# Unpermuted first chunk, one early load of the probabilities, first weights after the last q load, attention of later chunks moved up by six steps

## The chip, the cores and the metric

The kernel runs on one core of one Trainium2 chip. The metric is the device time of one execution in microseconds (us); the span in a profile, from the first to the last instruction, is 1.7 to 3.0 us shorter. Most executions agree within a per cent. Some come out 7 to 12 us later than the rest; they are called slow or late here, counted apart, and never used to explain a difference between fast ones.

## The reference

```python
# B=4, H=8, S=768, D=48; then N=3072 tokens, Din=384, E=4 experts, F=1024
f = 1.0 / (1.0 + np.exp(-f_logit))
for t in range(S):                      # gated linear attention
    state = f[:, :, t, :, None] * state + np.einsum('bhd,bhe->bhde', k[:, :, t], v[:, :, t])
    y[:, :, t] = np.einsum('bhd,bhde->bhe', q[:, :, t], state)
x = y.transpose(0, 2, 1, 3).reshape(B * S, H * D)
p = domain_probs / (domain_probs.sum(-1, keepdims=True) + 1e-09)
for e in range(E):                      # every expert, weighted by p
    out += p[:, e:e+1] * (np.maximum(x @ w1[e], 0.0) @ w2[e])
```

## The kernel before

The sequence is cut into 6 chunks of 128 steps. Each chunk goes through attention (gates, state sum "cs", products of q and k with exponentials, transposes, masked scores, y, transposed activations xT) and then through four experts of two layers. A list scheduler in Python simulates the engines with assumed durations, gives each step to an engine and fixes the order of all queues. The order on chip is what this simulation found.

```python
def load(c, nm, b, n):                                  # f, k, q, v: rows of 48 floats, 192 bytes
    ins[c, nm, b] = nc.sync.dma_start(out=tl(nm, c, b // 2)[:, hh(b, n), :], in_=srcs[nm][c, :, b * H:(b + n) * H, :])
def load_w(i, e, which):                                # expert weights, cast to bf16 on the way
    ins["w", i] = nc.gpsimd.dma_start(out=w[:, e], in_=r[e])
    if i == 0:
        after(ins["w", 0], ins[0, "k", B - 1])          # first weights wait for the first chunk's last k
# ... the first chunk's sixteen loads, in this order:
"f0 k0 q0 f1 k1 q1 f2 f3 k2 q2 v0 k3 q3 v1 v2 v3"
# ... tiles that stand ahead of the load buffers in SBUF:
pt = const.tile([128, B * C, E], FP32)                  # 384 bytes a partition
pn = const.tile([128, B * C, E], FP32)
psm = const.tile([128, B * C, 1], FP32)
# ... the plan's costs of a product (VectorE or GpSimd, whichever is free):
pe = {"DVE": 0.6, "POOL": 1.0} if c < 2 else {"POOL": 1.0}
```

## Time and profile before

| what | before |
|---|---|
| times | 301.59, 303.09 and 309.1 us, median 303.09 |
| span of the profiled execution | 300.35 us, clock 1.000 |
| first weights: issue, landing | 14.72, 23.05 us |
| head, up to the first expert matmul | 23.10 us |
| body, from there to the last matmul's end | 274.10 us |
| tail | 3.15 us |
| stops of TensorE in the body | 0.60 + 0.20 us at 80 to 82 us |

Head, body and tail add up to the span. A stop is a gap between the starts of two matmuls beyond what the first needs; gaps of 0.22 us that return regularly are lost records. The lines behind this table stand in the prediction.

### The profile page before, as it was taken

What the parts mean: (1) busy time and instruction counts of PE and PEld (TensorE: products, weight loads), DVE (VectorE), ACT (ScalarE), POOL (GpSimd) and SP (SyncE); (2) the same over time, 40 slices, a digit from 0 to 9 for tenths busy, and PEclk for the clock granted to TensorE, in tenths of its full rate; (3) what the DMA queues carried; (4) which work ended last, traced back from release to release, by engine and by line L of the source; (5) the groups of instructions that cost most, each with busy time, mean ns of one, the idle gap of its engine ahead of it and who ended that gap; (6) DMA issues with size and microseconds to landing.
All of it is one profiled execution on the core that took longest, in us unless ns stands there. A gap on an engine that the chain in (4) does not pass through costs nothing.

```text
span 300.4 us, 5514 instructions
## 1 busy us (share of the span) xinstructions
PE 290.7 (97%) x2111; PEld 168.1 (56%) x2141; DVE 135.8 (45%) x268; ACT 172.5 (57%) x300; POOL 95.7 (32%) x157
## 2 busy tenths in 40 slices
PE   7799999999999999999999999999999999999995
PEld 5564555567775565555555555555555555555553
DVE  6784013787852675516465325454415343201223
ACT  5766654858875455677355576445475444475440
POOL 4484400408756048423426243522432000000000
PEclk9999999999999999999999999999999999999999
DMA  7999999964994679969796978201322201200002
GB/s 155 210 180 206 207 207 200 220 103 71 224 208 103 119 142 180 196 136 156 152 177 116 241 147 153 49 21 34 94 58 52 48 13 41 75 4 2 0 0 105
DMA packets 137354, 36.08 MB, mean 120 GB/s; under 512 B 128496, under 2 KB 135792, under 8 KB 137328
## 3 DMA queue, kind: packets, MB, share of 16 engines
q1 hardware_dynamic: 131568, 29.45, 50.5%
q0 software_dynamic: 5760, 6.29, 12.6%
q8 instruction: 16, 0.26, 0.4%
q14 instruction: 10, 0.08, 0.1%
HBM read 31.51 MB, written 4.72 MB: 121 GB/s over the span
## 4 chain that ended last, share of the span: by engine, by line
PE 90%; DMA 4%; SPq 3%; DVE 1%; issue 1%
PE ps_m L356 42%; PE ps_m L344 41%; SPq L222 3%; DMA w_sb<-in_moe_w_dram 3%; PE ps_t L300 2%; DMA k<-in_k_dram 1%; PE ps_t L315 1%; PE ps_t L311 1%; PE ps_t L321 1%; PE ps_t L255 1%; PE ps_t L285 1%; DVE Sf L328 0%; DVE o L367 0%; DVE yb L218 0%; PE ps_t L340 0%
## 5 line engine op out<-in xcount | busy, mean ns | idle before, releaser
L356 PE MATMUL ps_m<-w_sb,h 128*128 128x384 bf16 x776 | 153.1, 324 | 0.2
L344 PE MATMUL ps_m<-xT,w_sb 128*128 128x512 bf16 (+1 forms) x594 | 150.8, 362 | 2.4 <-DMA w_sb<-in_moe_w_dram 0.5
L352 ACT ACTIVATE h<-ps_m 128x512 bf16<-128x512 f32 (+1 forms) x169 | 97.2, 577 | 96.5 <-PE ps_m L344 91.8
L356 PEld LDWEIGHTS <-h 128*128 128x128 bf16 x776 | 73.6, 98 | 58.7
L363 DVE SCALAR_TENSOR_TENSOR o<-ps_m,pn,o 128x384 f32<-128x384 f32 (+1 forms) x73 | 44.6, 611 | 107.3 <-PE ps_m L356 102.7
L344 PEld LDWEIGHTS <-w_sb 128*128 128x128 bf16 x624 | 59.5, 98 | 46.8 <-issue 0.8
L276 POOL TENSOR_TENSOR qk<-q,e 128x384 bf16<-128x384 f32 x19 | 22.8, 1202 | 67.3 <-ACT e L262 64.8
L335 POOL TENSOR_TENSOR Sf<-Sf,egs 48x192 f32<-48x192 f32 x40 | 20.1, 502 | 47.1 <-DVE Sf L328 45.1
L350 DVE TENSOR_SCALAR h<-ps_m 128x512 bf16<-128x512 f32 (+1 forms) x39 | 21.9, 578 | 27.6 <-PE ps_m L344 25.2
L304 DVE TENSOR_TENSOR AT<-ps_t,mask 128x512 bf16<-128x512 f32 x48 | 30.2, 682 | 6.8 <-PE ps_t L300 6.8
L276 POOL TENSOR_TENSOR qk<-k,e 128x384 bf16<-128x384 f32 x20 | 21.9, 1093 | 10.7 <-ACT egs L266 6.6
L262 ACT ACTIVATE e<-ps_t 128x384 f32<-128x384 f32 x24 | 20.8, 865 | 3.6 <-PE ps_t L255 2.5
L328 DVE TENSOR_TENSOR Sf<-Sf,ps_t 48x192 f32<-48x192 f32 x40 | 14.0, 350 | 8.3 <-PE ps_t L321 7.4
L336 POOL CAST sb<-Sf 48x192 bf16<-48x192 f32 x40 | 13.6, 339 | 2.6
L365 ACT ACTIVATE o<-ps_m,pn 128x384 f32<-128x384 f32 x20 | 11.6, 580 | 4.4 <-PE ps_m L356 3.2
L569 PE MATMUL ps_m<-busy 128*128 128x256 bf16 x69 | 12.1, 319 | 1.3 <-DVE busy L140 1.3
L264 ACT ACTIVATE e<-ps_t 128x384 f32<-128x384 f32 x24 | 13.0, 542 | 0.0
L247 ACT ACTIVATE ex<-f 128x768 f32<-128x768 f32 (+1 forms) x14 | 10.5, 750 | 4.4 <-DMA f<-in_f_logit_dram 4.4
L315 PE MATMUL ps_t<-vb,AT 128*128 128x48 bf16 x192 | 11.4, 184 | 1.0 <-DVE vb L218 1.0
L218 POOL CAST vb<-v 128x384 bf16<-128x384 f32 x18 | 9.4, 540 | 8.5 <-DMA v<-in_v_dram 7.3
L315 PEld LDWEIGHTS <-AT 128*128 128x128 bf16 x192 | 9.8, 97 | 3.1 <-issue 1.1
L251 ACT ACTIVATE gp<-ex 128x768 bf16<-128x768 f32 (+1 forms) x14 | 10.5, 752 | 0.4
(50 smaller groups left out, 134.5 us busy)
## 6 DMA issues: line engine op xcount, KB each, us to landing
w_sb<-in_moe_w_dram POOLq DMA_DIRECT2D x8, 768.0 KB, 18.9
out_dram<-o SPq DMA_DIRECT2D x23, 192.0 KB, 2.1
f<-in_f_logit_dram SPq DMA_DIRECT2D x10, 384.0 KB, 4.3
k<-in_k_dram SPq DMA_DIRECT2D x10, 384.0 KB, 5.5
q<-in_q_dram SPq DMA_DIRECT2D x10, 384.0 KB, 5.4
v<-in_v_dram SPq DMA_DIRECT2D x10, 384.0 KB, 5.1
f<-in_f_logit_dram SPq DMA_DIRECT2D x4, 192.0 KB, 4.0
k<-in_k_dram SPq DMA_DIRECT2D x4, 192.0 KB, 4.1
```

Of the source, the lines that this page charges most:

```text
L262: nc.scalar.activation(out=e[:, 0].rearrange("t (d h) -> t h d", d=D), in_=cs[:, 0:HD].rearrange("t (i r d) -> t r i d", r=2, d=D), func=A ...
L276: engines[eng].tensor_tensor(out=tl("qk", c, b)[:, j, :, 0:D].rearrange("t (i r) d -> t i r d", r=2), in0=tl("qk"[j], c, b // 2)[:, hh(b), ...
L304: nc.vector.tensor_tensor(out=tl("AT", c, b)[:, r].rearrange("s i t -> s (i t)"), in0=tl("A", c, b, r).rearrange("s i t -> s (i t)"), in1= ...
L315: nc.tensor.matmul(out=y[:, h * D:(h + 1) * D], lhsT=AT[:, r, i, :], rhs=vb[:, h, :], start=(c == 0), stop=True, skip_group_check=True)
L328: nc.vector.tensor_tensor(out=Sf[rows, b], in0=Sf[rows, b], in1=KV[rows, :, r, :], op=ALU.add)
L335: nc.gpsimd.tensor_tensor(out=Sf[rows, b], in0=Sf[rows, b], in1=eg, op=ALU.mult)
L336: nc.gpsimd.tensor_copy(out=nb[rows, b, :, r * D:(r + 1) * D], in_=Sf[rows, b])
L344: nc.tensor.matmul(out=tl("hp", c, e, fc, n0)[:, n0:n1], lhsT=w1_sb[:, e, kk, fc * 128:(fc + 1) * 128], rhs=tl("xT", c)[:, kk, n0:n1], sta ...
L350: nc.vector.tensor_relu(out=dst, in_=src)
L352: nc.scalar.activation(out=dst, in_=src, func=AF.Relu)
L356: nc.tensor.matmul(out=tl("op", c, e, nt, part)[:, cols], lhsT=tl("h", c, e)[:, fc, nt * T:(nt + 1) * T], rhs=w2_sb[:, e, fc, cols], start ...
L363: nc.vector.scalar_tensor_tensor(out=o, in0=op, scalar=pe, in1=o, op0=ALU.mult, op1=ALU.add)
```

## The change

The intent: finish the first chunk's attention earlier, keep the first weights out of the way of its last loads, take the small probability work out of the expert layers, and start later attention earlier.

```diff
-    pt = const.tile([128, B * C, E], FP32)
-    pn = const.tile([128, B * C, E], FP32)
-    psm = const.tile([128, B * C, 1], FP32)
+    NR = B * C
+    praw = const.tile([NR, T, E], FP32)            # 2048 bytes a partition
+    ident32 = const.tile([NR, NR], FP32)
+    pn = const.tile([T, E, NR], FP32)
+    psm = const.tile([T, NR], FP32)
@@ first weights
-            after(ins["w", 0], ins[0, "k", B - 1])
+            after(ins["w", 0], ins[0, "q", B - 1])
@@ probabilities: six loads by SyncE and six normalisations become one
+        nc.scalar.dma_start(out=praw, in_=moe_domain_probs.rearrange("(r p) e -> r p e", p=T))
+        for e in range(E):
+            nc.tensor.transpose(out=tl("pp")[:, e], in_=praw[:, :, e], identity=ident32)
@@ first chunk's exponential unpermuted
+        if c == 0:
+            nc.scalar.activation(out=e[:, 0], in_=cs[:, 0:HD], func=AF.Exp, scale=-1.0)
@@ the last batch's copies in parts (q/k, y and xT); here y
+            parts = [slice(0, KD)] if c or b < B - 1 else [slice(0, 2), slice(2, KD)]
@@ attention of chunks 4 to 6
-            base = u0 + (0 if c else 10)
+            base = u0 + {0: 10, 1: 0}.get(c, -6)
... (helpers, costs of the plan, lists of dependences: cut)
```

## The prediction

> **What bounds the kernel now.** I read the page's busy table first, then the sliced rows, the chain of waits, and the timeline around each place where TensorE stands still.
>
> ```profile
> PE 290.7 (97%) x2111; PEld 168.1 (56%) x2141; DVE 135.8 (45%) x268; ACT 172.5 (57%) x300; POOL 95.7 (32%) x157
> ...
> PE   7799999999999999999999999999999999999995
> ...
> PEclk9999999999999999999999999999999999999999
> DMA  7999999964994679969796978201322201200002
> ```
>
> TensorE is busy from the third slice to the end at full clock, every other engine is below 60%. But a busy PE need not be a useful one: the digits of the first three slices (to 22.5 us) are mostly filler matmuls on a tile "busy" that only keep the clock up. So there are three parts: a head until the first expert matmul, a body in which TensorE is the bound, and a tail.
>
> The chain of waits, cut to the head, says what the head waits for:
>
> ```profile
> 10.03 4.38 DMA k<-in_k_dram
> 14.72 8.33 DMA w_sb<-in_moe_w_dram
> 23.54 1.03 PE ps_m L344 x4
> ```
>
> The last k of the first chunk lands at 14.41; GpSimd, which waited for it, then issues the first expert weight slab, which lands at 14.72 + 8.33 = 23.05. The timeline of TensorE has the first expert matmul 0.05 us later:
>
> ```profile
> 21.68 0.34 PE L340 MATMUL ps_t<-ident,yb 128*128 128x128 bf16 x3
> 21.85 0.71 PE L569 MATMUL ps_m<-busy 128*128 128x256 bf16 x5
> 23.10 1.47 PE L344 MATMUL ps_m<-xT,w_sb 128*128 128x512 bf16 x5 [0.54 <-DMA w_sb<-in_moe_w_dram]
> ```
>
> The other condition, the last transposed activations (xT), is met at 22.53 (ACT copy at 22.05, 0.48 long). So the weights hold the end of the head, and attention is only 0.52 us behind them.
>
> The body: 6 chunks x 4 experts are 576 matmuls of 512 columns and 768 of 384. In the chain, four 384-column matmuls take 0.65 us (0.1625 each) and three 512-column ones 0.65 (0.216 each): 576 x 0.216 + 768 x 0.1625 = 249.2 us. From 23.10 to the end of the last matmul (297.2) are 274.1 us; the other 25 are attention's own matmuls for chunks 2 to 6. Going from start to start through TensorE's timeline I find, beside regular 0.22 us steps that are lost records (594 and 776 recorded where 624 and 768 or a few more were issued), just one real stop, of 0.6 us at 80.6:
>
> ```profile
> 79.59 0.17 DVE L241 TENSOR_REDUCE psm<-pt 128x4 f32<-128x16 f32 x1
> 79.80 0.17 DVE L242 TENSOR_SCALAR psm<-psm 128x4 f32<-128x4 f32 x1
> 80.01 0.18 DVE L243 RECIPROCAL psm<-psm 128x4 f32<-128x4 f32 x1
> 80.22 0.27 DVE L244 TENSOR_TENSOR pn<-pt,psm 128x16 f32<-128x16 f32 x1
> 80.52 1.14 DVE L367 TENSOR_SCALAR o<-ps_m,pn 128x384 f32<-128x384 f32 x2
> ...
> 81.19 1.01 PE L344 MATMUL ps_m<-xT,w_sb 128*128 128x256 bf16 x6 [0.43 <-DVE o L367]
> ```
>
> The second chunk's four small probability operations stand on VectorE ahead of the eviction that frees a PSUM buffer, and TensorE waits for that buffer. The tail, 297.2 to 300.4, is the last eviction and store.
>
> **What the Trainium skill says.** "PSUM — Partial Sum Buffer", section "Engine vs sequencer instructions": the queues of ScalarE, VectorE and GpSimd are strict FIFO. The lines above agree: the eviction at 80.52 stands behind 0.93 us of arithmetic on a few elements. "Advanced Engine Details and Errata", section "SBUF Cachelines": different 16-byte lines on each access cost time. The first chunk's exponential written in permuted order (a step of 32 bytes) takes 862 ns against 536 for the same size unpermuted, and the product that reads it permuted 856 on VectorE against 540: it agrees. "DMA: Bandwidth & Descriptors", section "Why small descriptors are slow (HBM only)": a packet carries a fixed overhead whatever its size. The 8 KB of one chunk's probabilities go as 512 rows of 16 bytes, and the transfer needs 10.5 us to land while the first weights move: no proof, but it agrees. "TensorE: Matmul & The Clock Gate", section "Wait — 56ns, not 53.3ns?": columns / 2.4 GHz plus 2.5 ns, so 162.5 and 215.8 ns; the trace agrees to the digit.
>
> **The change, part by part.**
> 1. First chunk unpermuted: 4 exponentials lose 0.33 us each on ScalarE, 4 q products 0.32 each on VectorE. Per batch the chain shortens by about 0.65 us. From arrival of the last q, VectorE is the pacing engine in this stretch (last mask product ends at 20.62).
> 2. Split copies for the last batch: the transposed q/k copy (1.01 us on ACT) becomes two of about 0.55, so the k half goes before q arrives; the y copy (0.54) and the xT copy (0.48) become two parallel parts, saving about 0.15 each. With 1, the last xT is ready at about 21.5 instead of 22.53 (estimate, adding the durations above behind the last q and v). That is 1.0 us off a path that is not the last one.
> 3. First weights now wait for the last q rather than the last k: those land at 15.32 and 14.41, so the issue slips by 0.9, and by about 0.25 more because the probabilities now go first (48 KB at some 200 GB/s). Against that: the old first slab moved its first packet at 16.62, while rows of v were still on the same 16 queues until about 17.1, and its packets took 0.7 to 0.8 us there instead of 0.172; and 512 probability packets of 22 ns, now gone, ran among it (some 400 before 22 us: 400 x 22 ns / 16 = 0.55 us). New sum, all from the packet records: issue 15.9, first packet 1.9 later at 17.8, about 0.6 of start-up, 340 packets at 100 per us = 3.4, so 21.9, and 0.3 to 1.0 until the slowest of the 16 engines has reported (one was held by an instruction fetch of 1.3 us at 16.1): **landing 22.2 to 22.9 or a little later, I take 22.7**, against 23.05. Gain 0.35.
> 4. The first state product of TensorE (4 matmuls of 96 columns, 0.17 us) now stands before the first expert matmul and falls into the wait for weights: 0.17 gained.
> 5. Probabilities: one load of 24 rows x 2 KB in the first microseconds on ScalarE's queue, four small transposes on TensorE where filler stood, and one normalisation for all chunks in the head in place of six. The operations between the chunks leave VectorE (5 x about 0.75 us). Only one of them was on the path: the 0.6 us stop goes.
> 6. Attention of chunks 4 to 6 moves up by six units of about 1.3 us. The order of instructions shows its matmuls some 8 us earlier against the expert ones; count and size are the same. TensorE had no stop there, so nothing is gained; the loads are placed at nearly the same points, so I expect no new wait.
> Sum: 0.35 + 0.17 + 0.6 = **1.1 us, 0.4%**; span 300.4 to 299.3.
>
> **Rivals.** (a) *The delayed weights become worse.* If the start-up of the weight queue takes as long as before (16.6 to 18.0) whatever else runs, the slab lands at 23.3 to 23.6 and the head loses 0.3 to 0.5, with the faster attention waiting in vain; total gain 0.3. For it: only 48 packets moved in those 1.4 us even after v had finished. Against: the packets were slowest during the overlap. (b) *Moved attention collides.* ScalarE and VectorE are fullest between 60 and 125 us (digits 7 and 8); if the fourth chunk's gates come before their logits land (the second half landed at 118.97 and was used at 118.99), ScalarE stops, evictions stop, and TensorE with four PSUM buffers stops after about 2 us. A cost of 1 to 4 us, per chunk at most. Against: in the new order these gates stand at the same place among the evictions. (c) *All of the head's gain counts*: if the weights land at 22.0, attention (21.5) nearly bounds, and the gain is 1.8. (d) *Nothing moves*, since a TensorE-bound body of 274 us is untouched: then only the run-to-run scatter is seen.
>
> **Range and chances.** The runs before are 301.59, 303.09 and 309.1, and the profiled one 302.06; 1.1 off a usual 302.5 is 301.4. The gain lies between -1 and 2, the scatter adds about 1: 299.8 to 303.6. To be 2% faster, 6 us would have to go, more than head wait, stop and tail together hold; to be 2% slower, rival (b) would have to strike repeatedly.
>
> **What would show it.** Right: first expert matmul at about 22.75, still released by the weight DMA, with xT ready a microsecond earlier; no stop of TensorE for an o eviction near 80; small probability operations once, near 22; filler fewer; tail unchanged; body equal within 0.5 us. Wrong: first expert matmul after 23.1 (rival a); TensorE gaps behind ScalarE's h evictions between 100 and 190 (rival b); first matmul released by an xT copy (step 2 undersized); a stop at 80 for another reason. The prediction as a whole fails if such a new wait exceeds 2 us.

## The result, and the profile after

After: 304.13, 304.1, 304.11, 304.67, 304.59 and 304.59 us, median 304.36. Before, in the same rounds: 301.59, 303.09, 301.85 and 301.91, with two slow ones of 309.1 and 312.73. The ratio is 1.0075, interval 1.0052 to 1.0098. A ratio is the mean time of one kernel's fast runs over that of the other's of the same rounds, so it is not quite the ratio of the medians. The change is correct, within 2%, and 0.75% slower, where 0.4% faster was predicted.

| profiled execution | before | after | difference | predicted |
|---|---|---|---|---|
| head | 23.10 | 23.80 | +0.70 | -0.35 |
| body | 274.10 | 275.14 | +1.04 | -0.77 |
| tail | 3.15 | 3.48 | +0.33 | 0 |
| span | 300.35 | 302.42 | +2.07 | -1.1 |

The page of the changed kernel shows the same picture of a TensorE-bound body: the sum cannot tell what went wrong.

```profile
PE 289.3 (96%) x2107; PEld 167.5 (55%) x2137; DVE 132.6 (44%) x252; ACT 169.3 (56%) x299; POOL 95.3 (32%) x158
...
PE   7689999999999999999999999999999999999995
...
PEclk9999999999999999999999999999999999999999
DMA  9999999992995659978999889601432000200002
```

**Head.** The chain of waits of the changed kernel (start, length, what) now goes through the last q load, which lands at 16.02, where the prediction had 15.57:

```profile
11.63 4.38 DMA q<-in_q_dram
16.02 0.30 issue
16.32 4.25 POOL w_sb L232 x5
```

Its TensorE timeline (start, length, operation, in brackets the idle time and what ended it) shows the state products (L328) ahead of the first expert matmul, as predicted, and that the weights still release it, but at 23.80:

```profile
22.05 0.53 PE L347 MATMUL ps_t<-ident,yb 128*128 128x128 bf16 x3
...
22.86 0.33 PE L328 MATMUL ps_t<-vb,qk 128*128 128x96 bf16 x4
23.80 1.47 PE L351 MATMUL ps_m<-xT,w_sb 128*128 128x512 bf16 x5 [0.61 <-DMA w_sb<-in_moe_w_dram]
```

**Body.** The stop at 80 is gone. The probability operations stand once on VectorE, in the head (first and last of the four):

```profile
22.76 0.25 DVE L245 TENSOR_REDUCE psm<-ps_m 128x24 f32<-128x96 f32 x1
...
23.59 0.26 DVE L248 TENSOR_TENSOR pn<-ps_m,psm 128x96 f32<-128x96 f32 x1
```

Elsewhere stand new stops: 0.34, 0.47 and 0.48 us at 58.5, 60.0 and 71.1, in the second chunk's attention and so ahead of the place of the old stop, and 0.74 at 145.5. With the state products that left the body (0.17), -0.17 - 0.80 + 1.29 + 0.74 = +1.06, the body's +1.04. This is the second chunk's part in the changed kernel:

```profile
57.68 1.19 POOL L283 TENSOR_TENSOR qk<-q,e 128x384 bf16<-128x384 f32 x1 [24.66 <-DMA q<-in_q_dram]
...
57.84 1.74 DVE L283 TENSOR_TENSOR qk<-q,e 128x384 bf16<-128x384 f32 x1
...
58.83 1.61 POOL L283 TENSOR_TENSOR qk<-k,e 128x384 bf16<-128x384 f32 x1
...
58.93 0.40 PE L292 MATMUL ps_t<-ident,qk 128*128 128x128 bf16 x4 [0.17 <-POOL qk L283]
...
59.63 0.39 PEld L292 LDWEIGHTS <-qk 128*128 128x128 bf16 x4 [0.15 <-DVE qk L283]
```

and in the kernel before, where no transpose waited:

```profile
55.96 2.65 POOL L276 TENSOR_TENSOR qk<-q,e 128x384 bf16<-128x384 f32 x2 [21.67 <-ACT e L262]
...
56.70 2.33 DVE L276 TENSOR_TENSOR qk<-k,e 128x384 bf16<-128x384 f32 x2
```

Two things differ: q comes in after the products could start (the first line waits for its DMA), and the second q product, which reads permuted, moved to VectorE, where it takes 1.74 us beside GpSimd. The later stop, in the changed kernel's timeline, is the prediction's rival b: ScalarE is idle until logits land, then TensorE until an eviction ends:

```profile
144.05 0.84 ACT L251 ACTIVATE ex<-f 128x768 f32<-128x768 f32 x1 [1.98 <-DMA f<-in_f_logit_dram]
...
146.31 0.81 PE L351 MATMUL ps_m<-xT,w_sb 128*128 128x512 bf16 x3 [0.58 <-ACT h L359]
```

**Tail.** After the last store has landed, 1.04 us remained before and 1.29 remain now. In the trace's records SyncE ends with 3 semaphore waits before and 8 after, some 0.06 us each.

### The profile page after: what moved, and what is told of

Read it like the earlier page. It is cut to its first block, busy times and chain, and to the rows that moved or that the text cites. A ratio compares the mean times of both kernels' runs of the same rounds, so it can differ in the third digit from the quotient of the medians.

```text
span 302.4 us, 5502 instructions
## 1 busy us (share of the span) xinstructions
PE 289.3 (96%) x2107; PEld 167.5 (55%) x2137; DVE 132.6 (44%) x252; ACT 169.3 (56%) x299; POOL 95.3 (32%) x158
## 4 chain that ended last, share of the span: by engine, by line
PE 77%; DMA 12%; SPq 5%; POOL 2%; issue 1%; DVE 1%; ACT 0%; POOLq 0%; DVEq 0%
PE ps_m L363 37%; PE ps_m L351 34%; DMA w_sb<-in_moe_w_dram 7%; SPq L225 5%; DMA q<-in_q_dram 4%; PE ps_t L307 2%; POOL w_sb L232 1%; PE ps_t L322 1%; PE ps_t L318 1%; PE ps_t L259 1%; PE ps_t L328 1%; POOL qk L283 1%; DVE qk L283 1%; PE ps_t L292 1%; PE ps_t L347 0%
## 5 line engine op out<-in xcount | busy, mean ns | idle before, releaser
L359 ACT ACTIVATE h<-ps_m 128x512 bf16<-128x512 f32 (+1 forms) x171 | 98.2, 577 | 100.3 <-PE ps_m L351 92.1
L351 PEld LDWEIGHTS <-w_sb 128*128 128x128 bf16 x624 | 59.9, 98 | 47.7 <-DMA w_sb<-in_moe_w_dram 0.8
L283 POOL TENSOR_TENSOR qk<-q,e 128x384 bf16<-128x384 f32 x18 | 21.4, 1186 | 54.9 <-DMA q<-in_q_dram 26.8
L357 DVE TENSOR_SCALAR h<-ps_m 128x512 bf16<-128x512 f32 (+1 forms) x37 | 20.9, 574 | 20.8 <-PE ps_m L351 19.9
L269 ACT ACTIVATE e<-ps_t 128x384 f32<-128x384 f32 x20 | 17.3, 865 | 3.1 <-PE ps_t L259 3.1
L271 ACT ACTIVATE e<-ps_t 128x384 f32<-128x384 f32 x24 | 12.8, 534 | 0.0
L583 PE MATMUL ps_m<-busy 128*128 128x256 bf16 x61 | 11.1, 306 | 1.3 <-DVE busy L140 1.3
```

Of the source, the lines that this page charges most:

```text
L269: nc.scalar.activation(out=e[:, 0].rearrange("t (d h) -> t h d", d=D), in_=cs[:, 0:HD].rearrange("t (i r d) -> t r i d", r=2, d=D), func=A ...
L283: engines[eng].tensor_tensor(out=tl("qk", c, b)[:, j, :, 0:D].rearrange("t (i r) d -> t i r d", r=2), in0=tl("qk"[j], c, b // 2)[:, hh(b), ...
L351: nc.tensor.matmul(out=tl("hp", c, e, fc, n0)[:, n0:n1], lhsT=w1_sb[:, e, kk, fc * 128:(fc + 1) * 128], rhs=tl("xT", c)[:, kk, n0:n1], sta ...
L357: nc.vector.tensor_relu(out=dst, in_=src)
L359: nc.scalar.activation(out=dst, in_=src, func=AF.Relu)
```

## The experiments

Seventeen kernels ran, all correct. Labels that begin with b_ are the kernel before with edits, all others the changed kernel with edits. A body, head or stop is that of one profiled execution; the times are of 4 to 8. "Packet" is the start of the first 16 KB packet of the page's queue "q8 instruction" after 5 us: it holds one of the 16 DMA engines for 1.0 to 1.4 us. "Last v" is how long SyncE's issue of its sixteenth load took, and when that load landed. "Late" counts executions 7 us or more over the rest.

| run | packet | last v: issue took, landed | weights wait for: issue, landing | first matmul | body | span | late |
|---|---|---|---|---|---|---|---|
| before | 16.1 | 0.90, 18.78 | k: 14.72, 23.05 | 23.10 | 274.10 | 300.4 | 6 of 48 |
| after | 15.2 | 2.28, 19.46 | q: 16.32, 23.75 | 23.80 | 275.14 | 302.4 | 0 of 6 |
| a_pad32 | 14.6 | 1.94, 18.66 | q: 17.07, 24.13 | 24.17 | 274.45 | 302.0 | 0 of 4 |
| b_pad1760 | 17.1 | 0.94, 19.95 | k: 15.16, 23.55 | 23.60 | 275.27 | 302.0 | 0 of 4 |
| a_base0 | 15.2 | 2.35, 19.46 | q: 16.21, 23.61 | 23.66 | 274.77 | 301.9 | 0 of 4 |
| a_pad32_base0 | 15.0 | 0.85, 18.48 | q: 15.73, 22.78 | 22.82 | 274.54 | 300.8 | 0 of 4 |
| a_prod | 14.8 | 2.33, 20.94 | q: 15.87, 23.23 | 24.70 | 275.26* | 303.4 | 0 of 6 |
| a_wk | 15.3 | 0.90, 18.77 | k: 14.55, 22.77 | 22.82 | 274.30 | 300.5 | 3 of 6 |
| b_probs (late) | 13.8 | 2.04, 28.17 | k: 14.63, 21.88 | 32.29 | 273.35 | 309.1 | 2 of 8 |
| a_sp | 14.5 | 2.02, 18.68 | q: 15.87, 24.95 | 25.42 | 274.48* | 303.3 | 0 of 6 |
| best (late) | 14.0 | 1.86, 27.98 | k: 14.73, 22.27 | 32.30 | 273.83* | 309.5 | 3 of 6 |
| best_shift (late) | 14.5 | 2.15, 28.74 | k: 14.67, 21.86 | 33.06 | 274.58* | 311.0 | 6 of 6 |
| b_probs_pin | 16.3 | 0.90, 18.98 | k: 14.82, 23.02 | 23.06 | 274.45 | 300.9 | 0 of 6 |
| b_wq | 14.1 | 1.92, 18.36 | q: 16.79, 23.81 | 23.86 | 275.00 | 302.0 | 0 of 6 |
| v_pool | 15.2 | 1.06, 18.61 | k, behind v: 15.68, 24.32 | 24.37 | 275.21* | 303.1 | 0 of 6 |
| v_pool_lag | 14.4 | 1.06, 18.79 | k, behind v: 16.16, 24.14 | 24.19 | 273.42 | 301.1 | 0 of 6 |
| a_full | 15.2 | 0.89, 18.72 | q: 15.45, 22.58 | 22.63 | 273.96 | 300.0 | 0 of 6 |
| a_full_lag | 14.5 | 1.99, 18.74 | q: 17.20, 24.40 | 24.45 | 273.41 | 301.3 | 0 of 6 |
| a_full_lag_egs | 14.3 | 2.11, 18.34 | q: 16.70, 23.70 | 23.75 | 273.41 | 300.6 | 0 of 6 |

(*) The first matmuls after the long wait ran at a reduced clock (0.51 granted from 24 to 26 us in a_prod); in a_prod this is worth 1.2 us. The chain of a_prod and that of a_wk show it, the same twelve matmuls each. In a_prod the weights had landed 1.5 us before the first matmul: it waited for attention, whose last v came at 20.94.

```profile
24.90 3.92 PE ps_m L352 x12
```

```profile
22.82 2.76 PE ps_m L352 x12
```

### Where the load buffers lie

The new tiles are 1760 bytes longer than the old ones, 27.5 times 64. So nearly all buffers of f, q, k and v, which started at a multiple of 64 bytes, start at 32 mod 64 after the change (and the other way round for two, the second buffers of f and of k). Two kernels tell whether that matters: the changed kernel with 32 bytes more, and the kernel before with 1760.

```diff
-    psm = const.tile([T, NR], FP32)                      # a_pad32
+    psm_w = const.tile([T, NR + 8], FP32)
+    psm = psm_w[:, 0:NR]
-    psm = const.tile([128, B * C, 1], FP32)              # b_pad1760, kernel before
+    psm_w = const.tile([128, B * C + 440, 1], FP32)
+    psm = psm_w[:, 0:B * C]
```

> The changed kernel with 32 bytes of padding after the probability tiles and nothing else. They move every load buffer from an address of 32 modulo 64 back to the remainder modulo 256 that it had in the kernel before. Theory LAYOUT: rows of 192 bytes that start at 32 modulo 64 cost the DMA more, so the loads of a half chunk (2048 rows) go from 2.14 us back to about 1.8, the last q of the first chunk lands at 15.3 to 15.6 instead of 16.02, the first expert matmul starts at 22.7 to 23.1 instead of 23.80, the stops of TensorE at 58 to 60 and 71 us go, and the time is 302.0 to 302.6 (the changed kernel: 304.4). Rival QUEUE (the probability load on ScalarE's queue, or the order of loads, slows the transfers): row times stay at 21 to 24 ns, time 304.0 to 304.7. Rival SHIFT (the moved attention costs it all): 304 as well.

> The kernel before with 1760 bytes of padding, which puts every load buffer at the very address that it has in the changed kernel (but for two that swap places); no instruction differs. LAYOUT: the loads become slow (2.1 us per half chunk), the first expert matmul moves from 23.1 to 23.6 to 24.0, and the time rises by 0.8 to 2 us, to 303.3 to 304.5. QUEUE and SHIFT: no change, 302.5 within 0.5.

The DMA view counts the packets of one core in a stretch. From 58.5 to 62.5 us each kernel moves nothing but these rows of 192 bytes; the kernel before, the changed one, b_pad1760 and a_pad32, in this order:

```profile
DMA packets 4576, 0.87 MB, mean 218 GB/s; under 512 B 4576, under 2 KB 4576, under 8 KB 4576
```

```profile
DMA packets 3930, 0.75 MB, mean 187 GB/s; under 512 B 3930, under 2 KB 3930, under 8 KB 3930
```

```profile
DMA packets 3917, 0.75 MB, mean 187 GB/s; under 512 B 3917, under 2 KB 3917, under 8 KB 3917
```

```profile
DMA packets 4610, 0.88 MB, mean 220 GB/s; under 512 B 4610, under 2 KB 4610, under 8 KB 4610
```

The rate follows the padding, whatever else the kernel does: 187 GB/s at 32 mod 64, 219 otherwise. In the packet records the same loads have a median of 20 to 24 ns a packet instead of 15 to 18, and half a chunk takes 2.11 us instead of 1.8. In b_pad1760, whose instructions are those of the kernel before, the first chunk's last q lands at 15.92 instead of 15.32, the head grows by 0.50 us and the span by 1.7 us, with 0.83 us of a new stop at 130 us. The times agree in direction but are too scattered to prove it (a_pad32 303.32, ratio 1.0016, interval 0.9963 to 1.0069; b_pad1760 303.85, ratio 1.0045, interval 0.9989 to 1.0101). a_pad32 keeps the shift by six steps and has no stop near 145, yet it lost the head: fifteen of the sixteen parts of q were in at 15.40, the last, which an instruction packet can have held (14.6), at 16.77. Its expectation that the stops at 58 to 71 us would go failed: 0.20, 0.47 and 0.47 us remained.

### The shift by six steps

```diff
-            base = u0 + {0: 10, 1: 0}.get(c, -6)
+            base = u0 + {0: 10, 1: 0}.get(c, 0)         # a_base0; a_pad32_base0 has the 32 bytes as well
```

> The changed kernel with the attention of chunks four to six at its old place, still at the shifted addresses. SHIFT: the stop of TensorE at 142 to 146 us (0.97 us, behind ScalarE that waits for f to land) goes, head and the stops at 58 to 71 stay; time 303.2 to 303.6. If the shift alone made the loss: 302. If late loads are the cause of that stop too, a stop of similar size stays or moves: 304.2.

> Both undone: addresses as before, attention at its old place; what stays is the first chunk's change and the early probabilities. If the two causes are separate and add: 301.0 to 301.8, so 0.7 to 1.5 us faster than the kernel before, the size that was predicted for the change. If it equals the padded kernel alone, the stop at 145 came from slow loads and not from the shift.

Without the shift the stop near 145 goes, as it does with the shift and the padding. So it takes both, and one profile of each is all there is. The late logits (issued 138.24, landed 144.03) had fast packets: all 2048 rows had started by 142. What came between is in the trace: an instruction packet from 141.87 to 143.05, and from 142.6 to 143.9 some 20 packets of the transposes that SyncE had issued just behind the load, which took 1.0 to 1.2 us each (their median is 0.018); fifteen of the load's sixteen parts landed at 143.93 or later. In a_pad32 the logits were in at 140.65, before that packet (141.64). That the packet held them is a coincidence in time that no run tests. In aligned kernels the shift is worth nothing (bodies 274.45 and 274.54). a_pad32_base0 met the prediction's head to 0.1 us: q at 15.42, weights at 22.78, first matmul at 22.82. But it kept stops of 0.24, 0.28, 0.46 and 0.47 us between 54 and 71 us. Times: a_base0 303.78 (ratio 1.0035, interval 0.9988 to 1.0081), a_pad32_base0 303.32 (1.0025, 0.9947 to 1.0103), where 301.0 to 301.8 was expected.

### The second chunk's products, the wait for k, the probabilities alone

Comparing the plans shows what the profile only hints at: in the changed kernel the simulation gave three of the four q products of the second chunk to the other engine than before. Four kernels:

```diff
+            pq, pk = (pe, pe) if c != 1 else ({"POOL": 1.0}, {"DVE": 0.6}) if b < B - 1 else ({"DVE": 0.6}, {"POOL": 1.0})
-            qm = P.add(f"q {c}.{b}", pe, ...             # a_prod = a_pad32_base0 with this
+            qm = P.add(f"q {c}.{b}", pq, ...             # (and pk for k)
-            after(ins["w", 0], ins[0, "q", B - 1])       # a_wk = a_pad32_base0 with this (and in the plan)
+            after(ins["w", 0], ins[0, "k", B - 1])
-        nc.scalar.dma_start(out=praw, ...                # a_sp = a_prod with this
+        nc.sync.dma_start(out=praw, ...                  # behind the sixteen loads
# b_probs: kernel before with praw, one normalisation, SyncE's load and the padding; nothing else of the change
```

> The changed kernel with the buffers of f, q, k and v back on the remainders they had before (32 bytes of padding), without the shift by six steps, and now also with the second chunk's products on the engines of the kernel before (q on GpSimd, k on VectorE; the last slice the other way round). Theory A (the schedule's reassignment makes the new stops): in the same kernel without this edit TensorE stopped 1.45 us in four places between 54 and 71 us for transposes of the second chunk's products, because VectorE took the permuted q product beside GpSimd and needed 1.63 us. Those stops go, the time from the first expert matmul to the last matmul falls from 274.5 to about 273.2 us, and the span to about 299.5 if the head is as in that run (first expert matmul 22.8). Rival B (the stops come from the earlier start of the second chunk, whoever computes the products): stops of the same sum stay, body 274.5. The end after the last store stays 1.28 us (probability load still issued by ScalarE).

> The same aligned kernel without the shift, products as the schedule gives them, but the first weights wait for the last k load as before the change, not for the last q load. Theory A (the wait for q only trades an earlier issue for undisturbed weights): issue about 14.7, landing 8.3 us later at about 23.0, first expert matmul 23.0 to 23.1, that is 0.2 to 0.3 later than the 22.8 of the run that waited for an early q (15.4), and 1.1 earlier than the one whose q landed at 16.8. Rival B (the landing is set by all bytes moved, whatever the order): 22.8 as with q. xT ready at about 22.5 in both. The stops at 54 to 71 us stay (1.4 us), body 274.5, span about 301.

> The kernel before with the probabilities part of the change alone (one early load of long rows, transposed on TensorE, one normalisation for all chunks), its load issued by SyncE instead of ScalarE, padded so that all buffers keep their remainders mod 64 (they move by 1792 bytes, 28 times 64); the schedule gives the second chunk's products to the engines of before. Theory A: the stop of 0.8 us at 80 to 81 goes and nothing else changes: head 23.1, body 273.3 to 273.5, end after the last store 1.03, span 299.5 to 299.8, faster than before by 0.2 to 0.3 per cent. Rival B (the stop only moves: the delay it stood for is paid in another place of the second chunk): body 274.1, span 300.3. If the end after the last store is 1.28 the ScalarE queue is not its cause.

> The aligned changed kernel without the shift, second chunk's products as before, and the probability load issued by SyncE after the loads of the first chunk. Theory A (the further DMA queue of ScalarE costs the 0.26 us at the program's end): end after the last store 1.03 instead of 1.28 us; otherwise as the run with ScalarE's queue: head 22.8 where q lands by 15.5, body 273.2, span about 299.2. Rival B (the end has another cause, as the o tiles or the compiler's program end): 1.28 stays. With all parts right this should be 1.0 to 1.3 us faster than before, 0.3 to 0.4 per cent.

**Products**: in a_prod the stops of 0.46 and 0.47 us are gone and 0.41, 0.16 and 0.13 remain: 0.70 in sum instead of 1.45. Less the reduced clock its body is about 274.1, so theory A held by half. The Trainium skill's "SBUF — State Buffer", section "SBUF: two separate sides", says that a VectorE operation with two SBUF inputs and a GpSimd operation that reads SBUF lock each other out for a whole instruction. The trace agrees: VectorE's q product above starts at 57.84, GpSimd's ends at 58.87, VectorE's ends 0.71 us after that (it takes 0.86 alone), and GpSimd's next then takes 1.61 us instead of the 1.00 that one took with no rival ahead of it. The plan's costs (0.6 and 1.0) know nothing of it.

**The wait for q** gains nothing: in a_wk the weights were issued 1.18 us earlier than in a_pad32_base0 and landed at the same time (22.77 and 22.78). Rival B held. But 3 of its 6 executions were late.

**SyncE's load** was a poor test: put last, it landed after 22 us, and TensorE waited 1.8 us for it in front of its transposes (a_sp 303.98, ratio 1.0059, interval 1.0025 to 1.0092). It settled the tail, though: 1.28 us after the last store with either queue, so ScalarE's queue is not the cause. All kernels with the one load have 1.27 to 1.36, b_wq (0.97) and b_pad1760 (0.98) have not. Why one load instead of six leaves more waits at the end was not tested. b_probs was profiled in a late execution, so its body, though as expected, decides nothing; its fast times (301.5 to 303.59, ratio 0.9986, interval 0.9965 to 1.0006) are those of before.

### Repairs together, and one part at a time

```diff
# best       = a_pad32_base0 with a_prod's and a_wk's edits;  best_shift = the same with the shift
# b_probs_pin = b_probs with ScalarE's load and a_prod's edit
-            after(ins["w", 0], ins[0, "k", B - 1])       # b_wq: kernel before with this one line
+            after(ins["w", 0], ins[0, "q", B - 1])
```

> The changed kernel with three repairs: buffers of f, q, k and v on the remainders of before, second chunk's products on the engines of before, first weights waiting for the last k load again; without the shift by six steps. Theory A (the losses found so far add up): first expert matmul 22.8 us as in the run without the products' repair (which had 22.82), body 273.2 (274.3 there, less stops of 0.46, 0.46 and 0.22), end after the last store 1.28; span 299.3, against 300.3 of before, 0.3 per cent faster. Rival B (the products' repair only moves the stops, as part of it seemed to in the two runs with it, which kept 0.5 to 0.7 us of stops between 60 and 75 us): body 273.8, span 299.9, hardly different from before. As the weights wait for k, some of its executions should be slow again.

> The same with the shift by six steps kept, that is the whole change with the three repairs. Theory A (the shift is worth nothing and costs nothing once loads are on time, as the two aligned runs without these repairs showed with bodies of 274.45 and 274.54): body and span within 0.2 us of the run without the shift, no stop of TensorE over 0.3 us between 100 and 290 us. Rival B (the earlier attention meets the loads of the fourth chunk again): a stop of 0.5 to 1 us near 142 to 146 us and a body 0.5 to 1 longer.

> The kernel before with the probabilities part alone, its early load issued by ScalarE as in the change, all buffers on the remainders of before, second chunk's products pinned to the engines of before. Theory A (this part is worth the stop of 0.8 us at 80 us, and pays about 0.25 at the end): first expert matmul 23.1, body 273.3 to 273.5, end after the last store 1.28, span 299.6 to 299.9. Rival B (the gain of the body is lost in the head, as transposes of probabilities come ahead of the first chunk's work on TensorE): first expert matmul 23.5 or later, span 300.3 or more.

> The kernel before with one line changed: the first weights wait for the last q load instead of the last k load; schedule, engines and buffers are untouched. Theory A (what arrives first is decided by the bytes ahead, so the wait moves the weights only if q is late): q lands near 15.3, weights issue near 15.6 and land at 22.8 to 23.1, first expert matmul 22.8 to 23.1 as before, span 300.0 to 300.3, no difference beyond 0.3 us. Rival B (the prediction's step 3): landing 22.7, first expert matmul 22.75, span 299.9 to 300.0. Rival C (a wait for q is a loss by itself): first expert matmul 23.5 or later, span over 300.7. The slow state: kernels with this wait had none in 30 executions so far, those with the wait for k about a quarter; if that is no chance, none of these six is slow.

b_probs_pin tells where its gain went: the stop at 80 is gone, and 0.62 us at 53.4, 0.32 at 59.9 and 0.30 at 57.0 take its place; the body is 0.35 longer, not 0.7 shorter (times 302.54, ratio 1.0021, interval 0.9987 to 1.0055). The first of these is the second chunk's state sum, which TensorE reaches before its gates (gp) are ready, as its timeline shows:

```profile
54.21 0.48 PE L259 MATMUL ps_t<-gp,Ub 128*128 128x384 bf16 x2 [0.46 <-ACT gp L255]
```

All three lie ahead of 80 us, so the removed stop cannot have caused them by letting TensorE arrive earlier. The order did: in b_probs_pin this state sum stands in TensorE's queue behind 157 of the expert layers' weight loads, in the kernel before behind 160, while its gates are ready at nearly the same time (54.15 and 53.98). The simulated schedule had moved it up.

b_wq lost 0.76 us in the head (q landed at 16.49; 303.23, ratio 1.0047, interval 1.0002 to 1.0092) and had another stop of 0.9 at 54.8: with late weights the second chunk's loads, which wait for them, are late too. So rival C's numbers came in that execution, but not from the wait alone: fifteen of q's sixteen parts were in at 15.26, the last at 16.49. Two of the six executions (302.07 and 302.11) were as fast as before.

best (fast executions 301.71 to 301.98, ratio 0.9988, interval 0.9956 to 1.0019) is level with before, and half of its executions are late; best_shift was late in all six (310.89 to 313.29), so its ratio of 1.0344 is late over fast and says nothing of the shift. Its expectation could not be tested. But the late profiles can be read. The chain of best:

```profile
13.93 14.05 DMA v<-in_v_dram
...
29.33 0.50 PE ps_t L348 x3
```

The last v load took 14 us. In the table, SyncE's last issue takes 0.85 to 0.94 us in the six runs in which the instruction packet starts after that issue has ended, and 1.86 to 2.35 in the eleven in which it starts earlier (v_pool and v_pool_lag issue this load elsewhere). Whether the packet lengthens the issue, or both have another cause, was not tested. In the second case the weights, if they wait for k only, are ahead of the v load. The Trainium skill's "DMA: Bandwidth & Descriptors", section "Queues, rings and completion order", says that each DMA engine takes turns between queues packet by packet; beside packets of 2 KB a v load of 192-byte rows gets little. The packet records agree: these 1024 rows took 9.8 us in best and 2.4 before. If the weights wait for q instead, they are held back with it, at a cost of about 1 us. So the wait for q is an insurance. The granted clock, low as well in late executions, followed the wait in the profiled ones: in best TensorE had no work from 20 us; the clock was still 1.00 until 22, and 0.50 from 24 to 32.

### A test of that account, and the repaired change

```diff
# v_pool = best, with the last v load in the weights' own queue ahead of them
+        if i == 0:
+            load(0, "v", B - 1, 1)                       # by GpSimd, after the last k
# v_pool_lag = v_pool with the plan told that the second chunk's loads land later
-                   deps=deps, takes=[(nm, c, b // 2)], lag=2.0)
+                   deps=deps, takes=[(nm, c, b // 2)], lag=2.8 if c == 1 else 2.0)
# a_full = the whole change with a_pad32's and a_prod's edits;  a_full_lag = the same with the later lag
-        "egs": ([MP, NP], FP32)                          # a_full_lag_egs = a_full_lag with 64-byte tiles,
+        "egs": ([MP, 4 * NP], FP32)                      # so that no load buffer lies at 32 mod 64
```

> The repaired kernel (remainders of before, products pinned, weights after the last k, no shift), with the last v load issued by GpSimd in the weights' queue, right ahead of the first weights, instead of by SyncE as its sixteenth load. Theory A (in the late executions the last v load was overtaken by the weights): none of the six executions is late (the same kernel without this edit had 3 of 6 at 311 to 313 us, the one with the shift 6 of 6); v lands by 18 to 19, weights about 1 us later than the 22.8 of a free run at most, first expert matmul 22.8 to 23.8, span 299.8 to 300.6. Rival B (the late executions have another cause, as the clock): again 2 to 6 of 6 late.

> The same, and the schedule told that the second chunk's loads land 0.8 us later than it assumed, which puts the second chunk's state sum some 0.65 us later into TensorE's queue. Theory A (part of the new stops is this sum queued ahead of its gates, as the stops of 0.24, 0.62 and 0.9 us near 54 us in three runs): no stop near 54 us, stops between 50 and 80 us under 0.5 us in sum, body 273.2 to 273.5, span 299.5 to 300. Rival B (moving it only moves the wait to the products or to the following state): stops of 0.5 to 1 us in sum as without the edit, body 273.8.

> The change as given (weights after the last q, shift by six steps, ScalarE's load), with only the 32 bytes of padding and the second chunk's products on the engines of before. Theory A (these two made the loss beyond the head's luck): body 273.2 to 273.8 instead of 275.1, no stop near 142 to 146 us, first expert matmul between 22.8 and 24.2 according to when q lands, span 299.5 to 301; no late execution. Rival B (the shift loses by itself): a stop near 142 to 146 us again, body over 274.5.

> The whole change (weights after the last q, shift by six steps, ScalarE's load of probabilities) with three repairs: 32 bytes of padding, second chunk's products on the engines of before, and the schedule told that the second chunk's loads land 0.8 us later. Theory A (the repairs add up): first expert matmul 22.6 to 22.9 where q lands by 15.5 (up to 24 where an instruction packet holds q's engine), body 273.2 to 273.6, end after the last store 1.29; span 299.4 in the good executions; median of the times 301.3 to 301.8, none late. Rival B (the shift by six steps takes the gain of the later placing): body 274 as without it.

> The same, with the eight small state-factor tiles padded from 32 to 64 bytes, so that no load buffer lies at 32 mod 64 any more (two of the eight buffers of f and k did in every kernel with fast loads). Theory A (a remainder of 32 mod 64 costs the load, as the packets showed): loads of k into the second buffer, 2.35 to 2.48 us per half chunk in the other aligned kernels where they run one after the other, come down to 1.7 to 1.85; in the head the loads of f2, f3, k2 and k3 come in 0.1 us shorter each, k3 lands at 14.2 or earlier, the weights and the first expert matmul 0.1 to 0.3 earlier; span 299.1 to 299.4. Rival B (the remainder mod 64 is not what matters): those loads stay as they are.

**Late executions**: v_pool and v_pool_lag have none in 12, with v at 18.6 and 18.8. Kernels that wait for q had none in 54; those that wait for k with v in SyncE's queue had 20 of 84, before included. That late executions come from the v load being overtaken is shown by the three late profiles (b_probs, best, best_shift) and by v_pool; the other late ones were not profiled. What sets the packet's time is not shown. As a version v_pool is no gain (304.18, ratio 1.0053, interval 1.0017 to 1.0088): the weights come later than expected and the head is 24.37. v_pool_lag is level with before (302.02, ratio 1.0008, interval 0.9977 to 1.0038).

**Later state sum**: v_pool_lag, a_full_lag and a_full_lag_egs have bodies of 273.42, 273.41 and 273.41, against 273.96 in a_full. Theory A held, 0.55 us; 0.2 of it are stops that went, the rest gaps too small to count as stops.

**The change with padding and pinned products** (a_full): head 22.63, no stop near 145, body 273.96 (273.2 to 273.8 was expected), span 300.0 and 0 of 6 late. Its timeline has the products back as before, and a small remaining wait:

```profile
55.76 2.65 POOL L284 TENSOR_TENSOR qk<-q,e 128x384 bf16<-128x384 f32 x2 [23.91 <-ACT e L270]
...
56.12 2.70 DVE L284 TENSOR_TENSOR qk<-k,e 128x384 bf16<-128x384 f32 x2
```

Other executions had spans up to 301.7, median time 303.46 (ratio 1.0033, interval 0.9997 to 1.0069).

**All together**: the two profiles of a_full_lag and a_full_lag_egs fell into executions with a late q (16.89 and 16.39), so heads of 24.45 and 23.75. In the best executions the span was 299.4 and 299.2; the kernel before had 299.8 in its best. In a_full_lag_egs the 2048 packets of the load of k into its second buffer, at 83 to 86 us, start within 1.67 us instead of 2.09 in a_full_lag, and k's first-chunk load into that buffer comes down to 15.8 ns a packet from 20.1: the remainder works in this direction too. Times: a_full_lag 302.31 (301.3 to 301.8 was expected; ratio 1.0013, interval 0.9982 to 1.0044), a_full_lag_egs 301.95 with all six between 300.92 and 302.4 (before 301.89; ratio 0.9994, interval 0.9976 to 1.0012). So no version was shown to be faster than the kernel before among fast executions. a_full_lag_egs is level with it there, and over all 48 executions of the kernel before, late ones in, the mean was 303.4.

## Why the prediction was wrong

The time came out at 304.36, above the range of 299.8 to 303.6. It stayed within 2% as predicted, but the direction was wrong. The span missed its forecast by 3.2 us: 1.05 in the head, 1.81 in the body, 0.33 in the tail.

1. **Step 3, the weights (wrong, the head's 1.05 us).** It took q's landing of the kernel before, 15.32, plus 0.25; in the changed kernel q landed at 16.02, and the slab then needed 7.43 us, not 6.8: 2.2 to its first packet instead of 1.9, and 0.9 of start-up instead of 0.6. The cause in this execution is that the buffers had moved by 27.5 times 64 bytes, which the prediction never looked at: the five loads from the first f's landing to the second q's took 5.24 us instead of 4.67, and b_pad1760 shows q 0.60 later from the padding alone. An instruction packet did not hold q here (its sixteen parts landed at 15.59 to 16.02), but it can, as a_pad32 and b_wq show. Where neither struck (a_full, a_pad32_base0), the landing was 22.58 and 22.78: the predicted 22.7. That it was met so closely is in part luck: q landed 0.15 to 0.43 earlier than predicted, and the slab took 7.05 to 7.13, so 6.8 was 0.3 short.
2. **Steps 1 and 2, xT at 21.5 (oversized).** It was ready at 22.84, and in aligned kernels with timely loads at 22.05 to 22.35 (21.75 in a_full_lag_egs): 0.2 to 0.8 gained, not 1.0. It did not bound the head in the result, but it does nearly in a_full.
3. **Step 4, state products (right)**: they ran in the wait, 0.17 us.
4. **Step 5, probabilities (right in itself, wrong in the sum).** The stop at 80 went, 0.80 us. What failed is that nothing else would change: with the whole change the simulated schedule put the second chunk's products on other engines and its attention at other places in TensorE's queue, and stops of 1.29 us came up at 58 to 71 us, ahead of the removed one. (The probabilities part alone, b_probs, left the products where they were.) In a_pad32_base0, pinning the products took 1.45 us of such stops down to 0.70 (a_prod). With the products pinned and the state sum later the body is 273.41, 0.69 below before, where 0.77 was predicted.
5. **Step 6, "no new wait" (wrong in this kernel).** Rival b struck once, for 0.74 us; without the shift, or with the padding, it did not. That the shift gains nothing was right.
6. **"Tail unchanged" (wrong)**: +0.33 us, of which 0.25 lie after the last store and come with the one load of probabilities.
7. **"Body equal within 0.5" (wrong)**: +1.04. Rival a, later weights, held, but not for its reason, the start-up of the weight queue: the first 48 packets took 0.9 us, before 1.6.

With the repairs, the predicted span of 299.3 was reached in single executions (299.4 and 299.2), 0.4 to 0.6 under the best of the kernel before (299.8), not 1.1; the fast executions as a whole are no faster. The parts were mostly right one by one; what was missing is that the same edit moved addresses and the schedule.

## What to carry to other kernels

When a change adds or resizes a tile, compare the addresses of all tiles behind it, and when a scheduler decides the order, compare its assignments, before blaming or crediting the edit itself. A stop that is removed counts only if the order of everything else stays; compare the places of the new stops with that of the old one before calling them its consequence. And a wait that costs a microsecond in the good executions may be there to keep another transfer from being overtaken in the bad ones.

## What the Trainium skill lacked or had wrong

- "DMA: Bandwidth & Descriptors" states no cost of the place of the destination in SBUF for small rows (the alignment that it prices is of what is read, at 256 bytes). Rows of 192 bytes from HBM moved at 187 GB/s into buffers at 32 mod 64 and at 218 to 220 GB/s into buffers at 0 mod 64 (half a chunk 2.11 against 1.8 us), shown in both directions by padding.
- "Runtime: NRT & Kernel Launch" has the instruction refills in blocks of 16 KiB, but no page gives what they cost data on the same engines: each of these packets in the head held one engine for 1.0 to 1.4 us, and SyncE's issue of the load that was under way took 1.86 to 2.35 us instead of 0.85 to 0.94. Where a load could then be overtaken by the weights, 20 of 84 executions came late, and the three of them that were profiled show it overtaken.
- No page gives a cost of the program's end by its pending waits: 8 instead of 3 semaphore waits on SyncE, 0.25 us more after the last store.
- "SBUF — State Buffer" has the lock between VectorE and GpSimd, but no duration for such a pair: a permuted q product of 0.86 us took 1.63 to 1.74 on VectorE beside GpSimd.
